# Decay attention and softplus feed-forward on one core: PSUM banks three and three, and the sign of the converted weights as a step of its own

## Chip, core and metric

The kernel runs on one core of a Trainium2 chip. The metric is the device time of one execution in microseconds; the lower the better. The engines are called as the profile calls them: PE (TensorE, with PEld for its weight loads), DVE (VectorE), ACT (ScalarE), POOL (GpSimd) and SP (SyncE, whose queue issues the DMAs).

## What is computed

Attention with a decay and a causal mask for 8 batches of 8 heads, 576 rows and 64 columns each, and then a feed-forward over the 4608 rows of 512 that come out of it:

```python
scores = scale * np.matmul(q, k.transpose(0, 1, 3, 2))
decay = cum[:, :, :, None] - cum[:, :, None, :]        # cum: running sum of log(clip(f))
scores = np.where(causal, -1000000000.0, scores + decay)
attn = softmax(scores)
x = np.matmul(attn, v)                                 # as 4608 rows of 512
h = x @ w_in                                           # 512 -> 2048
g = np.maximum(h, 0.0) + np.log1p(np.exp(-np.abs(h)))
out = g @ w_out                                        # 2048 -> 512
```

All in float32. Both weights arrive as 64-bit floats and are made into float32 in the kernel.

## The kernel before

**Order of work.** All instructions are first put into a list of operations, each with the engines that could do it, a nominal cost, what it must follow and which buffers or PSUM banks it takes and gives back. A planner (`Plan.run`) then goes through a window of 600 operations and always emits the one that can start earliest by its nominal costs. So each engine's order is fixed before the kernel runs. Where an operation may go to several engines, the planner takes the one with the smallest sum of start, cost and bias. Buffers and banks of one tag are given out in the order of the list; only the scores of attention (`loose`) may overtake, if a bank is left for the one that they pass. Where PE would stand idle for over 0.5 us before the first feed-forward accumulation, the planner puts in matmuls that nobody reads (`fill_gap`, tile `fill`, L1219).

**Weights** (`load_f64`). 32 pieces of 128x512: 16 of `w_in` (tiles `ti`, results in `woh`) and 16 of `w_out` (tiles `to`, results in `wol`). A piece is loaded (L416, 512 KB) into one of five staging buffers, of which only the two of tag `wl` serve the last twelve pieces; ACT scales its high words (L420) into a buffer of tag `fe` (four of them); POOL or DVE clips that (L423; nominal 1.57 us on POOL, and 0.34 us with a bias of 1.0 on DVE); DVE then shifts it left by three bits (L427), joins the upper bits of the low words (L431, after which the staging buffer is free for the next load) and joins the sign bit (L435, after which `fe` is free). The loads stand in SP's queue between those of q, k and v (L586 to L642).

**Attention.** Twelve jobs on plain float32 come first (four with the first 256 rows of two heads, eight with the rest of the first batch), then 56 heads in split precision. A head takes twelve PSUM banks of tag `att`: six for tiles of scores `s` (L725, L726; then DVE finds the row minimum, L730, and ACT the exponential, L750, which gives the bank back), four for turned weights `b` (L805; copied to `ph`, and DVE's L820 gives the bank back) and two for products with v, `o` (L859; given back by L886).

**Feed-forward.** 16 blocks of 256 rows and two of 512. The first works on plain float32 (L996, L1100) beside the twelve plain jobs. A unit of 512 columns of `h` fills one bank of tag `h` (L1016), goes through ACT (L1052 to L1058) and DVE (L1066), is split into `gh` and `gl` (L1074 gives the bank back), and two units later the second product runs (L1107) into banks of tag `acc`. The last two blocks use two `att` banks as well. The plain block keeps its values in buffers of tag `gh`, of which there are three, until their second product is done. Of the eight PSUM banks, `att` has four, `h` two and `acc` two.

Of the kernel before, what the change touches and what calls it, by code (L numbers as in the profile page):

```python
# [10 lines left out]
F32 = mybir.dt.float32  # L11
U32 = mybir.dt.uint32
F32R = mybir.dt.float32r
AF = mybir.ActivationFunctionType
ALU = mybir.AluOpType
# [29 lines left out]
class Plan:  # L45
# [13 lines left out]
    def add(self, on, emit, after=(), takes=(), lag=None, loose=False):  # L59
        op = Op(on, emit, after, takes, lag)  # L60
        op.loose = loose
        op.at = len(self.ops)
        self.ops.append(op)
        for t in set(takes):
            self.queue[t].append(op)
        for d in op.after:
            d.users.append(op)
        return op

    def give(self, tag, ops):  # L70

        left = [len(ops), 0.0]
        for op in ops:
            self.gives.setdefault(op, []).append((tag, left))
# [89 lines left out]
def on_act(n, more=0.0, psum=False):  # L164
    return On("ACT", (0.067 if psum else 0.095) + n / 1200 + more)


def on_dve(n, fast=False, port=False, bias=0.0):
    return On("DVE", 0.071 + n / (1920 if fast else 960), bias, fast or port)
# [39 lines left out]
def tile_decay_attention_softplus_ffn(  # L209
# [21 lines left out]
    P = 128  # L231
# [8 lines left out]
    LAG = 2  # L240
# [2 lines left out]
    QT = [(0, 64)] + [(64 + 128 * i, 128) for i in range(4)]  # L243
    QF, QR = [(0, 128), (128, 128)], [(256, 64), (320, 128), (448, 128)]

    BUFS = dict(T=2, att=4, h=2, acc=2, xs=1, fe=4, ph=3, pl=3, ph64=2, pl64=2, gh=LAG + 1, gl=LAG + 1, xh=1, xl=1,
                x32=2, wl=2, vhl=3, vraw=2, raw=1)
    plan = Plan(BUFS | dict(T0=4, stat=4, p=2, x0=1, x1=1, x2=1))
    add, give = plan.add, plan.give

    def add_dma(emit, kb, n=1, eng="SP", **more):
        return add(on_dma(kb, n, eng), emit, lag=dma_lag(kb, n, eng), **more)
# [6 lines left out]
    def bank(tag, name):  # L259
        return psum.tile([P, 512], F32, tag=tag, name=name, bufs=BUFS[tag])  # L260

    def buf(tag, shape, name, dtype=F32):
        return pool.tile(shape, dtype, tag=tag, name=name, bufs=BUFS[tag])

# [6 lines left out]
    T = {}  # L271
# [124 lines left out]
    def load_f64(src, new, name, takes=()):  # L396


        at = count["w"]
        count["w"] += 1  # L400
        stag = STAGE[at % len(STAGE)] if at < 20 else "wl"

        tag = {"xh0": "x0", "xh1": "x1", "xl0": "x2"}.get(stag, stag)
        box = {}

        def load(e):
            if stag == "wl":
                s = buf(stag, [P, NCC, TB], f"st{name}", F32R)
            else:
                x = stag[:2]  # L410
                if x not in stage_of:
                    stage_of[x] = buf(x, [P, 2, NCC, TB], f"{x}_st", F32R)
                s = stage_of[x][:, int(stag[2])]
            box["s"] = s.bitcast(U32)
            box["s"] = box["s"].rearrange("p a b -> p (a b)").rearrange("p (c t) -> p c t", t=2)
            e.dma_start(out=box["s"], in_=src)  # L416

        def scale(e):
            box["t"] = buf("fe", [P, 512], f"t{name}")
            e.activation(box["t"], box["s"][:, :, 1].bitcast(F32), AF.Copy, scale=2.0**-112)  # L420

        def clip(e):
            e.tensor_scalar(box["t"], box["t"], -HIGH, HIGH, ALU.max, ALU.min)  # L423

        def shift(e):
            x = box["x"] = new().bitcast(U32)
            e.tensor_scalar(x, box["t"].bitcast(U32), 3, None, ALU.logical_shift_left)  # L427

        def low(e):
            x, lo = box["x"], box["s"][:, :, 0]  # L430
            e.scalar_tensor_tensor(x, lo, 29, x, ALU.logical_shift_right, ALU.bitwise_or)  # L431

        def sign(e):
            x, h = box["x"], box["t"].bitcast(U32)
            e.scalar_tensor_tensor(x, h, 0x80000000, x, ALU.bitwise_and, ALU.bitwise_or)  # L435

        ld = add_dma(load, 512, after=first_rows, takes=(tag,))
        sc = add(on_act(512, 0.04), scale, after=[ld], takes=("fe",))
        on = [On("POOL", 1.57), on_dve(512, True, bias=SCALE_BIAS)]
        bt = add(on, clip, after=[sc])  # L440
        bt = add(on_dve(512, True), shift, after=[bt], takes=takes)
        bt = add(on_dve(512, port=True), low, after=[bt])
        give(tag, [bt])
        bt = add(on_dve(512, port=True), sign, after=[bt])
        give("fe", [bt])
        return bt

    def piece(x, i, dtype=F32):
# [3 lines left out]
    def load_w_in(i):  # L452
        def new():
            w_in32[i] = piece("woh", i)
            return w_in32[i]

        cc, fq = i % NCC, i // NCC
        src = w_in[cc * P : (cc + 1) * P, fq * 512 : (fq + 1) * 512]
        w_in_ready[i] = load_f64(src, new, f"i{i}")

    def load_w_out(i):
        def new():
            w_out32[i] = buf("gl", [P, DM], f"wol{i + 1}") if i == NFC - 1 else piece("wol", i + 1)
            return w_out32[i]

        takes = ("gl",) if i == NFC - 1 else ()
        w_out_ready[i] = load_f64(w_out[i * P : (i + 1) * P], new, f"o{i}", takes)
# [724 lines left out]
    att = [attention(j) for j in jobs] + [nothing, nothing]  # L1192
# [118 lines left out]
```

## Time and profile before

| | us |
|---|---|
| median of 3 runs | 1237.31 (1235.45 to 1237.55) |
| the profiled execution | 1236.16 |
| its span in the profile | 1234.4 |
| PE busy | 1214.8 (98%) |
| DVE busy | 869.1 (70%) |
| ACT busy | 870.4 (71%) |
| POOL busy | 156.5 (13%) |

Busy times of PE are made of matmuls that overlap, so 98% does not say that PE has no gaps; its `fill` matmuls count as busy as well. The stages by time: up to about 63 us the first plain jobs and two thirds of the weights, up to about 200 us the rest of the plain work, up to about 1005 us the heads in split precision with the feed-forward between them, and after that the feed-forward alone.

### The profile page before, as it was taken

The page shows a single profiled execution, that of the slowest core. Times are in us where ns is not written, and L with a number is a line of the kernel's source. Part 1 is how long each engine was busy: PE and PEld are TensorE (multiplying, and loading weights), DVE is VectorE, ACT ScalarE, POOL GpSimd, SP SyncE. Part 2 cuts the span into 40 slices and gives each one's busy share as a digit, 9 for nine tenths or more (in the row PEclk, how much of TensorE's full clock was granted, in tenths as well). Part 3 has the DMA queues.
Part 4 walks back from the last instruction along what each step waited for, and adds up shares of the span by engine and source line. Part 5 has one row for each costly group of instructions (what it writes and reads, how often), then busy time and mean ns, then how long its engine had stood idle before and what let it go on. Part 6 is the DMA issues. An engine that isn't in the chain of part 4 may idle for free.

```text
span 1234.4 us, 21512 instructions
## 1 busy us (share of the span) xinstructions
PE 1214.8 (98%) x7648; PEld 1066.9 (86%) x7648; DVE 869.1 (70%) x2175; ACT 870.4 (71%) x2069; POOL 156.5 (13%) x130
## 2 busy tenths in 40 slices
PE   8899999999999999999999999999999999999998
PEld 6666678898999999999999999999988999888887
DVE  7898999998887887676777677777778852323322
ACT  5577788978887777676776778677878754444543
POOL 4742011110110111010111001100010100000000
PEclk9899999999999999999999999999999999999999
DMA  7864534443354334343433444334434223211210
GB/s 223 262 176 133 153 92 145 128 123 119 110 152 116 121 109 117 112 130 111 118 119 95 135 118 136 99 114 118 136 102 134 73 69 103 68 52 51 86 52 35
DMA packets 53355, 143.33 MB, mean 116 GB/s; under 512 B 6656, under 2 KB 21016, under 8 KB 53248
## 3 DMA queue, kind: packets, MB, share of 16 engines
q1 hardware_dynamic: 53248, 141.95, 38.5%
q8 instruction: 61, 1.00, 0.4%
q14 instruction: 46, 0.38, 0.1%
HBM read 127.85 MB, written 14.07 MB: 115 GB/s over the span
## 4 chain that ended last, share of the span: by engine, by line
PE 74%; DVE 13%; ACT 5%; DMA 3%; issue 2%; POOL 1%; SPq 1%; DVEq 0%; ACTq 0%; POOLq 0%
PE h L1016 28%; PE acc L1107 27%; PE o L859 6%; PE b L805 6%; PE s L725 3%; PE s L726 3%; DVE s L730 2%; ACT p L773 2%; ACT p L750 1%; DMA raw<-in_qkT 1%; DVE pl L820 1%; PE acc L1100 1%; POOL ti L423 1%; DVE T L681 1%; DMA xl_st<-in_w_out 1%
## 5 line engine op out<-in xcount | busy, mean ns | idle before, releaser
L1016 PE MATMUL h<-xh,wih 128*128 128x256 f32 (+1 forms) x960 | 277.2, 312 | 0.8 <-DVE gl L1074 0.8
L1016 PE MATMUL h<-xl,wih 128*128 128x256 f32 (+1 forms) x960 | 262.9, 297 | 0.0
L1107 PE MATMUL acc<-woh_dt_float32r,gh 128*128 128x512 f32 x544 | 221.8, 408 | 0.0
L750 ACT ACTIVATE p<-s,negm 128x288 f32<-128x288 f32 (+7 forms) x384 | 183.0, 479 | 50.2 <-DVE negm L730 47.7
L1107 PE MATMUL acc<-woh_dt_float32r,gl 128*128 128x512 f32 x544 | 213.4, 392 | 0.0
L1107 PE MATMUL acc<-wol_dt_float32r,gh 128*128 128x512 f32 x544 | 213.0, 391 | 0.0
L1066 DVE SCALAR_TENSOR_TENSOR h<-h,e 128x512 f32<-128x512 f32 x136 | 95.2, 701 | 152.4 <-ACT e L1058 151.9
L775 POOL TENSOR_SCALAR p<-p,rsum 128x448 f32<-128x448 f32 (+4 forms) x77 | 97.7, 1275 | 754.7 <-DVE rsum L764 476.3
L1016 PEld LDWEIGHTS h<-xh,wih 128*128 128x128 f32 x960 | 182.7, 190 | 7.3 <-DVE gl L1074 1.2
L1016 PEld LDWEIGHTS h<-xl,wih 128*128 128x128 f32 x960 | 183.0, 191 | 5.8
L730 DVE CUSTOM_DVE_ANT_0 s<-s,cmask 128x288 f32<-128x288 f32 (+5 forms) x320 | 137.2, 438 | 54.7 <-PE s L726 46.6
L1016 PE MATMUL h<-xh,wl 128*128 128x256 f32 (+1 forms) x960 | 167.9, 297 | 0.0
L1052 ACT ACTIVATE e<-h 128x512 f32<-128x512 f32 x144 | 85.7, 595 | 111.5 <-PE h L1016 109.6
L820 DVE TENSOR_TENSOR pl<-b,ph 128x512 fp32r<-128x512 f32 (+1 forms) x224 | 125.9, 569 | 41.7 <-ACT ph L205 39.5
L805 PE MATMUL b<-ident,p 128*128 128x128 f32 x960 | 147.0, 277 | 7.9 <-ACT p L773 4.2
L1016 PEld LDWEIGHTS h<-xh,wl 128*128 128x128 f32 x960 | 138.4, 190 | 4.9
L805 PEld LDWEIGHTS b<-ident,p 128*128 128x128 f32 x960 | 112.7, 141 | 27.6 <-ACT p L773 6.5
L773 ACT ACTIVATE p<-p,rsum 128x576 f32<-128x576 f32 (+7 forms) x221 | 105.8, 542 | 28.8 <-DVE rsum L764 28.6
L1107 PEld LDWEIGHTS acc<-woh_dt_float32r,gl 128*128 128x128 f32 x544 | 102.2, 188 | 22.7
L1074 DVE TENSOR_TENSOR gl<-h,gh 128x512 fp32r<-128x512 f32 x136 | 93.6, 688 | 34.8 <-ACT gh L205 33.4
L1107 PEld LDWEIGHTS acc<-wol_dt_float32r,gh 128*128 128x128 f32 x544 | 102.9, 189 | 15.0
L1107 PEld LDWEIGHTS acc<-woh_dt_float32r,gh 128*128 128x128 f32 x544 | 102.8, 189 | 15.0
(107 smaller groups left out, 2142.8 us busy)
## 6 DMA issues: line engine op xcount, KB each, us to landing
wl<-wil_d SPq DMA_DIRECT2D x120, 512.0 KB
raw<-in_qkT SPq DMA_DIRECT2D x112, 288.0 KB
vr<-in_vR SPq DMA_DIRECT2D x64, 160.0 KB
out<-ob SPq DMA_DIRECT2D x36, 256.0 KB
sto<-in_w_out SPq DMA_DIRECT2D x11, 512.0 KB
sti<-in_w_in SPq DMA_DIRECT2D x9, 512.0 KB
wil_d<-wil SPq DMA_DIRECT2D x16, 256.0 KB
xh_st<-in_w_in SPq DMA_DIRECT2D x5, 512.0 KB
```

The lines of the kernel that those rows point to most:

```text
L730: e.tensor_tensor_reduce(out=box["o"], in0=box["o"], in1=cmask[0:n_q, right - w : right], scale=-0.125, scalar=m0 if i else 3.0e38, op0=AL ...
L750: e.activation(o, box["o"], AF.Exp, bias=m1, scale=-1.0, accum_out=acc)
L773: e.activation(a, a, AF.Copy, scale=f_)
L775: e.tensor_scalar(a, a, f_, None, ALU.mult)
L805: e.transpose(box["ps"][:, at : at + P], pt[pi][:, c : c + P], ident)
L820: e.tensor_sub(box["l"], box["ps"][:, pad : pad + w], box["h"].bitcast(F32))
L859: e.matmul(box["ps"][:, a - g0 : z - g0], st["vhl"][:, vc, :], pbox[x][:, o : o + z - a], start=i == 0 and m == 0, stop=i == len(todo) - 1 ...
L1016: e.matmul(o, l, r, start=m == 0, stop=m == 11)
L1052: e.activation(box["e"], view(st["h", fp]), AF.Abs)
L1066: e.scalar_tensor_tensor(h, h, 0.0, box["e"], ALU.max, ALU.add)
L1074: e.tensor_sub(box["l"], box["t"], box["h"].bitcast(F32))
L1107: e.matmul(st["acc"][tt], l, r[fc], start=fc == 0 and m == 0, stop=fc == NFC - 1 and m == 2,)
```

## The change

`att` gets three banks in place of four and `h` three in place of two. In the conversion of a weight piece the sign is prepared before the shift: a new step multiplies the clipped value by zero, which leaves a zero of the value's sign, in a buffer of tag `gh`. It may go to POOL or DVE with the same nominal costs as the clip. The shift then takes both tensors and joins the sign in the same instruction, and the last join is gone. `fe` and `gh` are free after the shift, the staging buffer after the join of the low words, which is now the last step.

```diff
-    BUFS = dict(T=2, att=4, h=2, acc=2, xs=1, fe=4, ph=3, pl=3, ph64=2, pl64=2, gh=LAG + 1, gl=LAG + 1, xh=1, xl=1,
+    BUFS = dict(T=2, att=3, h=3, acc=2, xs=1, fe=4, ph=3, pl=3, ph64=2, pl64=2, gh=LAG + 1, gl=LAG + 1, xh=1, xl=1,
...
+        def sign(e):
+
+            box["z"] = buf("gh", [P, 512], f"z{name}", F32R).bitcast(F32)
+            e.tensor_scalar(box["z"], box["t"], 0.0, None, ALU.mult)
+
         def shift(e):
             x = box["x"] = new().bitcast(U32)
-            e.tensor_scalar(x, box["t"].bitcast(U32), 3, None, ALU.logical_shift_left)
+            t, z = box["t"].bitcast(U32), box["z"].bitcast(U32)
+            e.scalar_tensor_tensor(x, t, 3, z, ALU.logical_shift_left, ALU.bitwise_or)
...
-        def sign(e):
-            x, h = box["x"], box["t"].bitcast(U32)
-            e.scalar_tensor_tensor(x, h, 0x80000000, x, ALU.bitwise_and, ALU.bitwise_or)
...
         bt = add(on, clip, after=[sc])
-        bt = add(on_dve(512, True), shift, after=[bt], takes=takes)
+        bt = add(on, sign, after=[bt], takes=("gh",))
+        bt = add(on_dve(512, port=True), shift, after=[bt], takes=takes)
+        give("fe", [bt])
+        give("gh", [bt])
         bt = add(on_dve(512, port=True), low, after=[bt])
         give(tag, [bt])
-        bt = add(on_dve(512, port=True), sign, after=[bt])
-        give("fe", [bt])
```

## Rows read from the trace of the kernel before

**Rows 1.** Busy time by stage: window, sum, engines (instructions), clock, DMA share, GB/s.

```profile
18.00:63.00 45.00, 38.93 (x234) 30.49 (x232) 40.95 (x97) 28.89 (x72) 29.92 (x19) 0.89 0.88 278
63.00:120.00 57.00, 55.98 (x249) 36.26 (x248) 51.02 (x135) 42.02 (x101) 20.36 (x11) 1.00 0.52 157
200.00:250.00 50.00, 48.74 (x353) 44.68 (x352) 48.61 (x130) 43.08 (x115) 6.89 (x5) 1.00 0.45 130
300.00:900.00 600.00, 599.29 (x4184) 556.03 (x4183) 449.39 (x1141) 457.61 (x1112) 64.68 (x49) 1.00 0.40 117
```

**Rows 2.** PE's unread matmuls from 18 to 63 us, groups of instructions by line.

```profile
L1219 PE MATMUL fill<-cmask 128*128 128x128 f32 x152 | 21.9, 296 | 0.0
```

**Rows 3.** Chain that ended last, from 20 to 60 us: start, length, what.

```profile
29.57 2.12 POOL to L423
...
35.09 0.60 DVE wol_dt_float L431
```

**Rows 4.** DVE's groups from 18 to 120 us: busy, mean ns, idle before.

```profile
L435 DVE SCALAR_TENSOR_TENSOR woh_dt_float<-ti,woh_dt_float 128x512 uint32<-128x512 uint32 x16 | 10.9, 685 | 0.1
...
L427 DVE TENSOR_SCALAR wol_dt_float<-to 128x512 uint32<-128x512 uint32 x15 | 7.8, 527 | 2.2 <-POOL to L423 2.2
L427 DVE TENSOR_SCALAR woh_dt_float<-ti 128x512 uint32<-128x512 uint32 x16 | 6.9, 444 | 2.4 <-POOL ti L423 2.4
```

**Rows 5.** The clip's line over the span: duration least/median/most in ns.

```profile
L423 POOL TENSOR_SCALAR to<-to x12: 1911/2067/2200, 27.4 to 111.2; 128x512 f32<-128x512 f32 x12
L423 POOL TENSOR_SCALAR ti<-ti x10: 1913/2121/2434, 18.8 to 100.5; 128x512 f32<-128x512 f32 x10
L423 DVE TENSOR_SCALAR ti<-ti x6: 411/423/884, 21.9 to 96.0; 128x512 f32<-128x512 f32 x6
L423 DVE TENSOR_SCALAR to<-to x4: 418/422/504, 51.8 to 115.8; 128x512 f32<-128x512 f32 x4
```

**Rows 6.** DVE's waits for the clip: total us, times, longest.

```profile
DVE woh_dt_float L427 <- POOL ti L423: 2.4, 4, 0.9
DVE wol_dt_float L427 <- POOL to L423: 2.2, 3, 1.4
```

**Rows 7.** Timeline: start, us, engine, line, instruction.

```profile
26.82 0.41 DVE L427 TENSOR_SCALAR woh_dt_float<-ti 128x512 uint32<-128x512 uint32 x1
27.43 8.09 POOL L423 TENSOR_SCALAR to<-to 128x512 f32<-128x512 f32 x4 [1.41 <-DVE woh_dt_float L427]
27.75 1.09 DVE L431 SCALAR_TENSOR_TENSOR woh_dt_float<-xh_st,woh_dt_float 128x512 uint32<-128x512 uint32 x1
...
87.81 0.49 DVE L763 TENSOR_SCALAR lsum<-lsum 128x3 f32<-128x3 f32 x1
```

**Rows 8.** PE's waits over the span: total us, times, longest.

```profile
PE s L725 <- ACT p L750: 3.2, 3, 1.4
...
PE b L805 <- ACT p L750: 2.0, 7, 0.4
...
PE h L1016 <- DVE gl L1074: 0.8, 2, 0.5
```

**Rows 9.** Timeline: first product with v of the first and the tenth head.

```profile
152.52 0.49 PE L859 MATMUL o<-ph,vhl 128*128 128x320 f32 x1
...
258.00 0.31 PE L859 MATMUL o<-ph,vhl 128*128 128x320 f32 x1
```

**Rows 10.** Timeline: one turned bank and one tile of scores, taken and given back.

```profile
225.62 0.77 PE L805 MATMUL b<-ident,p 128*128 128x128 f32 x5
226.14 0.38 PE L725 MATMUL s<-T 128*128 128x288 f32 x1
...
227.73 0.68 DVE L820 TENSOR_TENSOR pl<-b,ph 128x512 fp32r<-128x512 f32 x1
...
229.60 0.50 ACT L750 ACTIVATE p<-s,negm 128x288 f32<-128x288 f32 x1
```

**Rows 11.** SP's waits before a weight load: total us, times, longest.

```profile
SPq L416 <- DVE wol_dt_float L431: 29.7, 11, 6.2
```

## The prediction

> **What bounds the kernel now.** I read the busy times by stage first, then the chain that ended last, then the waits of the engines, and the timeline where a wait needed its cause.
>
> The stages have different limits [rows 1]. From 300 to 900 us PE is busy for 599.29 of 600 us: neither the banks nor the weights can gain much there, but they can lose. From 18 to 63 us PE's 38.93 us are in good part not work: 21.9 us of them are matmuls that nobody reads [rows 2]. In that stage DVE is busy for 40.95 of 45 us and the DMA engines for 0.88 of it. From 63 to 120 us DVE has 51.02 of 57 us and from 200 to 250 us 48.61 of 50 us. The chain between 20 and 60 us runs over the conversion of the weights, on DVE and on POOL [rows 3]. So up to 300 us DVE's time is what counts, and in the first 63 us a delay or a gain shows as more or less `fill`.
>
> **The weights, step by step.** There are 32 pieces, all converted between 18 and 120 us.
>
> Removed from DVE: 32 shifts in their short form. They take 7.8 + 6.9 us for 31 of them [rows 4], 15.1 us with the last one; 0.41 us each where nothing disturbs them [rows 7], 13.1 us in all. The shift in its new form reads two tensors, as the join of the sign at L435 does, which goes; the one replaces the other at 0.68 us each [rows 4], and the sum of the two is zero.
>
> Added: 32 multiplications by zero, of the clip's form, so at the clip's price: 2.07 to 2.12 us on POOL, 0.42 us on DVE [rows 5]. What the planner gives to which engine I take from the clips and from POOL's free time. Of the clips POOL got 22 of 32 [rows 5]. From 18 to 63 us POOL is busy for 29.92 of 45 us [rows 1]: 15.1 us are free, room for 7 more. From 63 to 120 us 36.6 us are free, room for all of the 13 pieces of that stage; at the share of the clips 9 go there. That makes 16 signs on POOL and 16 on DVE. The ends are all on POOL and all on DVE.
>
> DVE's saving before any side effect: 13.1 - 16 x 0.42 = 6.4 us; 13.1 us with all on POOL, and -0.3 us with all on DVE.
>
> The side effect that decides: POOL's work costs DVE time. The join at 27.75 us takes 1.09 us, where such an instruction takes 0.68 us, and it begins 0.32 us after the start of a clip on POOL [rows 7]. I count 13 such DVE instructions, of five lines, beside the 22 clips on POOL, from that one to the one at 87.81 us [rows 7]; each is 0.32 to 0.45 us longer than its like, 5.4 us together, or 0.25 us for each POOL instruction. Sixteen more on POOL cost DVE 4.0 us (32: 7.9 us; none: 0). The join at 27.75 us ended at 28.84 us, while the clip beside it, the first of four that took 8.09 us, ran to about 29.45 us [rows 7]: it waited for a part of the POOL instruction, not for its end. The Trainium skill, "SBUF — State Buffer", section "Who interferes with whom", says otherwise: whichever of a GpSimd instruction that reads SBUF and a VectorE instruction with two inputs there comes first has the shared port pair for its whole length, and the other is blocked until it ends. No row here shows so long a block; the rule's own result is the fifth rival.
>
> The second side effect: DVE waits for POOL. It did so for 2.4 + 2.2 us at L427 with 22 instructions on POOL [rows 6], 0.21 us each; 16 more make 3.3 us. The reason is that the clip's nominal price is 1.57 us and the real one 2.07 us or more: DVE's order is set by the first, and what stands behind the waiting shift in DVE's order, row minima and normalisations of the plain jobs, waits too, with PE behind them. Ends: 0 (all on DVE) and 6.7 us (all on POOL).
>
> Sum for the weights: -6.4 + 4.0 + 3.3 = +0.9 us. All on POOL: -13.1 + 7.9 + 6.7 = +1.5 us; all on DVE: +0.3 us; side effects that fall where DVE would have stood idle: down to -6.4 us.
>
> Moved with it: the staging buffer is free only after the last step, so each of the 27 later loads is issued later, by the new step's time less nothing that is gone ahead of it, up to 2.1 us. Behind a waiting load in SP's queue stand the loads of q, k and v and the decay rows of the plain jobs. SP waited for a free staging buffer for 29.7 us at the `w_out` pieces alone [rows 11] without the chain going through it for long, so I cost it at nothing; if that cover is gone, it is part of the third rival. The `gh` buffers for the signs: three, one or two of which the plain feed-forward block holds from 74 us on; a sign holds one for some 3 us (2.07 us plus the shift), pieces of that time come 57 / 13 = 4.4 us apart, so one is enough: nothing.
>
> **The banks.** What a bank costs now is seen in PE's waits [rows 8]. For the release of an `att` bank by the exponential PE waited 3.2 us at new scores and 2.0 us at turned weights, for the release of an `h` bank 0.8 us. Three in place of four for `att`: with the same queueing the first two grow by a third, 1.7 us; from below nothing, as the planner can put feed-forward matmuls there; I take 1.0 us. Three for `h`: the 0.8 us can go. Between them +0.2 us. The upper bound for `att` comes from its holding time between 150 and 260 us: ten heads begin 9 intervals apart from 152.52 to 258.00 us, 11.7 us each [rows 9]. A tile of scores held its bank from 226.14 to 230.10 us, a turned bank from 225.62 to 228.41 us [rows 10]. With 2.8 us for the products with v as well, a head holds 6 x 3.96 + 6 x 2.8 = 40.6 us of bank time, 3.5 of the four banks on the mean. Three banks give that in 13.5 us per head, 1.8 us more; for the 13 heads to 300 us that is +23 us at most. What speaks against it: the banks are held so long because their tiles queue for DVE, which is busy for 48.61 of 50 us there [rows 1]; with fewer tiles in the queue each is held for less. I take the low end, as DVE's busy share is the nearer row.
>
> **Sum.** The profiled execution took 1236.16 us (span 1234.4 us and 1.8 us around it). +0.9 and +0.2 us give 1237.3 us; the median lies 1.15 us above that execution, so the forecast is 1238.4 us, or no change that can be measured. About 0.2% is what a measurement of this kernel can tell from no change. The forecast's own range is 1234 to 1241 us.
>
> **Rivals.**
>
> First, faster: the planner, which sees 6.4 us less on DVE, orders the first 63 us better, and the stretched instructions fall beside the chain. Then 6.4 us and up to two of the 3.3 us of waits are won: 1237.3 - 6.4 - 1.5 = 1229.4 us. For it: 21.9 us of `fill` to be won, and DVE on the chain. Against it: POOL is on the chain as well [rows 3].
>
> Second, faster: the third `h` bank lets PE run feed-forward matmuls wherever attention is late. PE's idle time by the rows of its stages is 1.0 us from 63 to 120 us and 1.3 us from 200 to 250 us [rows 1], so some 2% of the 180 us from 120 to 300 us and a like share of the last heads, 6 us in all: 1231.3 us. Against it: only 0.8 us of waits on `h` are seen.
>
> Third, slower: POOL sets the pace of the first stage. If the planner gives POOL both steps of each of the 14 pieces that it clips up to 63 us, that is 28 x 2.1 = 58.8 us in a stage of 45 us, 13.8 us too much; DVE's order waits for half of it, as the other half lies beside DVE's own work: 1244.3 us. It decides from the point where POOL's free 15.1 us are used up, 7 signs. For it: the nominal price, which is 0.5 us too low for each instruction. Against it: the planner turns to DVE when POOL has a queue.
>
> Fourth, slower: the three `att` banks do stretch the heads from 150 to 300 us. A third of the upper bound is 8 us: 1245.3 us. It decides where the mean need of banks, 3.5, stays above three. For it: the 5.2 us of waits on `att` with four banks. Against it: DVE's queue, as said.
>
> Fifth, slower: a POOL instruction keeps a DVE instruction with two inputs waiting until it ends. The shift is now such an instruction, and the joins are. One that begins at a random point of a sign waits 1.0 us, half of 2.07 us; 16 of them cost 16.6 us in place of 4.0 us: 1251.0 us. Against it: the 13 stretched instructions wait 0.45 us at most. This is the rule of the Trainium skill's page on SBUF named above.
>
> That the change doesn't do what it says could only be that the planner puts nearly all signs on DVE; that is in the forecast's range.
>
> **How the numbers follow.** Forecast 0.30, first rival 0.25, second 0.10, third 0.14, fourth 0.18, fifth 0.03. Within 0.2% of 1237.31 us (1234.8 to 1239.8 us) lies most of the forecast, with 0.02 of it below and 0.01 above: faster 0.37, same 0.27, slower 0.36. The range that should hold the time 8 times in 10 takes in the centres of the first four rivals, and stops short of both faster ones together (1223 us) and both slower ones together (1251 us): 1226 to 1248 us.
>
> **What would show it.** Right: the multiplications by zero some half on POOL and half on DVE; 15 to 25 DVE instructions stretched by 0.3 to 0.5 us before 120 us; DVE's waits for POOL of 6 to 10 us; `fill` from 18 to 63 us at about 22 us; the heads from 150 to 260 us still under 12 us apart; from 300 us on PE as full as now. The first rival is seen in `fill` under 16 us and an earlier start of the plain feed-forward; the second in less idle PE time from 120 to 300 us; the third in `fill` over 27 us with DVE waiting for POOL at the new shift; the fourth in heads of 12.5 us or more and more of PE's waits on L750. Wrong it would be above all if the planner's new order moves the plain jobs against the weights by more than the terms here, since each engine's order is made anew by any change of cost.

## The result and the profile after

Over seven runs of each on the same chips the kernel before took 1236.66 us (median, 1235.45 to 1238.41) and the changed kernel 1239.77 us (1238.41 to 1241.7): a ratio of 1.0028 with an interval of 1.0018 to 1.0038. The change costs 0.28%, a little more than the 0.2% that can be told from nothing. All times are medians of executions with a mean granted clock of 0.99 or more; one execution each of e2_sign and d2_att2 and one of the kernel before ran at 0.75 to 0.85 and are left out. The profiled execution of the changed kernel has a span of 1238.0 us (before 1234.4 us) with a mean granted clock of 0.997 (before 0.994); from 300 to 900 us it is 1.00 in both. Line numbers behind the new step are three higher than before (L725 is L728, L750 is L753, L805 is L808).

Busy time by stage in the changed kernel, to be laid beside [rows 1] with the same columns:

```profile
18.00:63.00 45.00, 39.34 (x225) 29.89 (x225) 42.80 (x96) 32.42 (x84) 34.66 (x23) 0.94 0.86 257
63.00:120.00 57.00, 55.87 (x243) 35.79 (x242) 51.21 (x132) 39.95 (x94) 22.17 (x14) 1.00 0.56 173
200.00:250.00 50.00, 49.59 (x337) 44.29 (x336) 44.57 (x122) 41.91 (x108) 6.40 (x5) 1.00 0.44 125
300.00:900.00 600.00, 598.27 (x4150) 551.00 (x4151) 453.41 (x1149) 460.83 (x1129) 65.42 (x51) 1.00 0.41 118
```

The first column, PE's busy time, has hardly moved anywhere. The loss is in the last row, and in the columns beside it: from 300 to 900 us there are 34 matmuls fewer (4150 in place of 4184) and 5.0 us less of weight loads (551.00 in place of 556.03 us), while "busy" fell by 1.0 us only. At 600 us for 4184 matmuls, 34 of them are 4.9 us on the mean, more than the 3.6 us by which the span grew.

The unread matmuls from 18 to 63 us, to be laid beside [rows 2]:

```profile
L1222 PE MATMUL fill<-cmask 128*128 128x128 f32 x131 | 20.7, 302 | 0.0
```

The clip (L423) and the new sign step (L428) by engine, to be laid beside [rows 5] (least, median and most ns of one):

```profile
L423 DVE TENSOR_SCALAR ti<-ti x10: 414/428/875, 18.7 to 98.3; 128x512 f32<-128x512 f32 x10
L423 DVE TENSOR_SCALAR to<-to x10: 408/428/878, 29.1 to 120.4; 128x512 f32<-128x512 f32 x10
L423 POOL TENSOR_SCALAR to<-to x6: 1926/2114/2294, 33.9 to 73.4; 128x512 f32<-128x512 f32 x6
L423 POOL TENSOR_SCALAR ti<-ti x6: 1923/2264/2460, 43.6 to 101.5; 128x512 f32<-128x512 f32 x6
...
L428 POOL TENSOR_SCALAR zo<-to x10: 1488/1746/1980, 30.0 to 121.0; 128x512 f32<-128x512 f32 x10
L428 DVE TENSOR_SCALAR zi<-ti x9: 407/427/823, 19.3 to 103.6; 128x512 f32<-128x512 f32 x9
L428 POOL TENSOR_SCALAR zi<-ti x7: 1488/1497/1860, 23.5 to 98.9; 128x512 f32<-128x512 f32 x7
L428 DVE TENSOR_SCALAR zo<-to x6: 407/427/828, 36.3 to 116.6; 128x512 f32<-128x512 f32 x6
```

Signs: 17 on POOL, 15 on DVE. But of the clips POOL now has 12 in place of 22. POOL's conversion work is 29 instructions in place of 22, not 38, and DVE has 35 of the short ones (20 clips, 15 signs) in place of 42 (10 clips, 32 short shifts).

DVE's waits for POOL from 18 to 125 us, beside [rows 6] (total us, times, longest):

```profile
DVE zi L428 <- POOL ti L423: 1.4, 1, 1.4
DVE wol_dt_float L433 <- POOL zo L428: 0.9, 2, 0.5
DVE woh_dt_float L433 <- POOL zi L428: 0.5, 1, 0.5
DVE zo L428 <- POOL to L423: 0.2, 1, 0.2
```

PE's waits over the span on the banks, beside [rows 8], and the first product with v of the first and of the tenth head, beside [rows 9]:

```profile
PE b L808 <- ACT p L753: 3.5, 9, 0.8
...
PE s L726 <- ACT p L753: 1.4, 3, 0.9
...
PE h L1019 <- DVE gl L1077: 0.2, 1, 0.2
```

```profile
157.77 0.39 PE L862 MATMUL o<-ph,vhl 128*128 128x320 f32 x1
...
275.34 0.39 PE L862 MATMUL o<-ph,vhl 128*128 128x320 f32 x1
```

The heads now begin 117.57 / 9 = 13.06 us apart; before it was 11.72 us.

### An account of PE's time

"Busy" does not show what is lost, because a matmul's record runs on while the next one has begun. The distance from one start to the next does. This is the timeline of PE in the changed kernel (start, us, engine, line, instruction):

```profile
336.39 0.28 PE L1019 MATMUL h<-xh,wih 128*128 128x256 f32 x1
336.51 0.28 PE L1019 MATMUL h<-xl,wih 128*128 128x256 f32 x1
336.80 0.39 PE L728 MATMUL s<-T 128*128 128x320 f32 x1
```

The first distance, 0.12 us, is that of such a matmul when nothing stops it. The second is 0.29 us: 0.17 us went by before the scores could begin, and all but 0.01 us of it hides in a "busy" of 0.28 us. I did this for every matmul of the span: its distance to the next start, less the distance of its kind in the kernel before when undisturbed (the one that a fifth of them stay below; for the single-precision kinds the median). What is left is called a gap here. `fill` is the distance that the unread matmuls take up. Span less `fill` less gaps comes out at 1127.4 to 1128.5 us in all kernels below, so the two account for their differences to about 1 us. In us:

```
kernel        att/h sign step  span    fill  gaps 0-63  63-300  300-900  900 on
before         4/2   no        1234.4  37.9     4.6      24.6     28.3    10.7
e2_sign        4/2   yes       1232.1  28.5     6.8      29.8     28.5    10.1
s1_sign_dve    4/2   DVE only  1235.3  38.3     3.8      25.7     28.3    10.7
n1_lag         4/2   no        1238.5  39.9     2.6      28.2     28.6    11.0
n2_sign_lag    4/2   yes       1236.0  28.5     8.4      31.8     28.3    10.7
n5_lag2        4/2   no        1231.3  38.0     4.4      22.3     28.5     9.8
after          3/3   yes       1238.0  35.4     4.9      24.5     34.8    10.4
e1_banks       3/3   no        1243.8  40.1     4.1      26.8     35.0    10.2
n3_banks_lag   3/3   no        1238.4  39.9     3.4      22.1     35.4     9.9
n4_both_lag    3/3   yes       1242.4  44.9     3.7      20.9     34.6    10.1
e3_att3        3/2   no        1246.7  39.1     4.5      29.8     35.3    10.6
e4_sign_att3   3/2   yes       1239.7  35.9     4.8      25.1     35.2    10.8
```

Each row is one profiled execution; with the 1.8 us around its span it lies up to 2.2 us from the median of its kernel, so differences of 2 us between two rows alone prove little. Between before and after: +6.5 us from 300 to 900 us, -2.5 us of `fill`, and 0.3 us or less elsewhere. The size hangs a little on what is taken as undisturbed: with the median for every kind the same step is +5.7 us, with the distance that a tenth stay below +7.9 us. Three and four banks stand apart with each of them.

The two kernels do not run the same mix in that stretch. As the heads come later, the changed kernel has 1575 matmuls of attention there in place of 1536, and 2575 of the feed-forward in place of 2645. That is not what makes the gaps: at the gaps of before after a matmul of each sort the new mix would have 0.5 us less of them. What grew is the gap after a matmul of scores, from 7 to 14 ns on the mean.

### The profile page after: what moved, and what is told of

The parts are those of the page before. It is cut to its first block, busy times and chain, and to the rows that moved or that the text cites. A ratio compares the mean times of both kernels' runs of the same rounds, so it can differ in the third digit from the quotient of the medians.

```text
span 1238.0 us, 21502 instructions
## 1 busy us (share of the span) xinstructions
PE 1217.8 (98%) x7622; PEld 1062.6 (86%) x7622; DVE 873.2 (71%) x2159; ACT 875.7 (71%) x2080; POOL 162.4 (13%) x135
## 4 chain that ended last, share of the span: by engine, by line
PE 76%; DVE 13%; ACT 4%; DMA 3%; issue 2%; POOL 1%; SPq 0%; DVEq 0%; POOLq 0%; ACTq 0%
PE h L1019 28%; PE acc L1110 27%; PE b L808 7%; PE o L862 6%; PE s L728 3%; PE s L729 3%; DVE s L733 2%; ACT p L776 1%; DVE T L684 1%; ACT p L753 1%; DVE T L690 1%; DMA sto<-in_w_out 1%; DVE pl L823 1%; DMA sti<-in_w_in 1%; DMA raw<-in_qkT 1%
## 5 line engine op out<-in xcount | busy, mean ns | idle before, releaser
L753 ACT ACTIVATE p<-s,negm 128x288 f32<-128x288 f32 (+7 forms) x384 | 182.9, 479 | 56.3 <-DVE negm L733 54.9
L808 PE MATMUL b<-ident,p 128*128 128x128 f32 x960 | 142.4, 275 | 6.9 <-ACT p L753 3.5
L808 PEld LDWEIGHTS b<-ident,p 128*128 128x128 f32 x960 | 111.6, 140 | 28.9 <-ACT p L753 8.7
L776 ACT ACTIVATE p<-p,rsum 64x64 f32<-64x64 f32 (+6 forms) x226 | 107.4, 539 | 29.4 <-DVE rsum L767 28.4
```

What stands on the lines that cost most here:

```text
L753: e.activation(o, box["o"], AF.Exp, bias=m1, scale=-1.0, accum_out=acc)
L776: e.activation(a, a, AF.Copy, scale=f_)
L808: e.transpose(box["ps"][:, at : at + P], pt[pi][:, c : c + P], ident)
```

## The experiments

Two explanations stood against each other at first: that the banks cost time and the sign step gives some back, or that neither does much and the planner's new order decides. The planner makes one list of all engines' instructions from nominal costs, so any edit changes the order of everything behind it.

### One part alone

**e1_banks**: the kernel before with the new bank counts only.

```diff
-    BUFS = dict(T=2, att=4, h=2, acc=2, ...
+    BUFS = dict(T=2, att=3, h=3, acc=2, ...
```

> Three attention banks and three banks for the first product, with the weights converted as before. Bank theory (the attention banks stretch the heads up to 300 us): the first ten heads 13.1 us apart as in the changed kernel, fill from 18 to 63 us as before (21.9 us), time 0.4% to 0.6% over before, 1241 to 1244 us. Sign theory (the conversion costs the time): no change, heads 11.7 us apart. Order theory (any new order of the instructions moves the time by some us either way): a time within 0.4% of before that says nothing of either part.

Measured: 1244.82 us, a ratio of 1.0074 (1.0062 to 1.0086). The banks alone cost 0.7%, more than the whole change. The bank theory is the nearest of the three, but the heads are further apart than it said (14.0 us in place of 13.1 us) and the time lies just above its range.

**e2_sign**: the changed kernel with the old bank counts.

```diff
-    BUFS = dict(T=2, att=3, h=3, acc=2, ...
+    BUFS = dict(T=2, att=4, h=2, acc=2, ...
```

> The new conversion of the weights alone, with four attention banks and two for the first product. Bank theory: heads 11.7 us apart as before, fill 2 to 3 us less, time 0.2% under before, some 1234 us. Sign theory: slower than before by about what the whole change costs, 1240 us, with DVE waiting for POOL. Order theory: within 0.4% of before, either way.

Measured: 1236.00 us, 1.0003 (0.9994 to 1.0012). The sign step alone does nothing that can be measured, and the sign theory falls with it. The bank theory's details do not hold here: the heads are 12.4 us apart, and `fill` falls by more than the 2 to 3 us that it said. The windows of the two, in the columns of [rows 1]; first the banks alone:

```profile
200.00:250.00 50.00, 44.27 (x292) 40.01 (x291) 41.90 (x111) 36.65 (x93) 3.33 (x4) 0.93 0.40 123
300.00:900.00 600.00, 598.31 (x4153) 550.87 (x4153) 453.47 (x1157) 461.32 (x1132) 66.97 (x52) 1.00 0.39 117
```

then the sign step alone:

```profile
200.00:250.00 50.00, 45.55 (x310) 40.83 (x309) 44.05 (x123) 38.94 (x104) 7.00 (x6) 0.97 0.39 114
300.00:900.00 600.00, 599.27 (x4176) 555.32 (x4174) 448.91 (x1142) 457.80 (x1111) 65.83 (x50) 1.00 0.39 118
```

From 300 to 900 us the banks alone do what the changed kernel does, 4153 matmuls and 550.87 us of weight loads; the sign step alone leaves both nearly as they were. So the loss behind 300 us belongs to the banks. Ahead of 300 us the sign step alone won 9.4 us of `fill`:

```profile
L1222 PE MATMUL fill<-cmask 128*128 128x128 f32 x96 | 13.1, 286 | 0.0
```

(21.9 us in [rows 2]), and lost most of it again: gaps grew by 2.2 us up to 63 us and by 5.2 us from there to 300 us. The chain that ended last, of the sign step alone, from 195 to 255 us (start, length, what), shows where: 25.5% of it are loads of q and k for a next head into the single `raw` buffer.

```profile
198.84 5.05 DMA raw<-in_qkT
...
238.73 5.95 DMA raw<-in_qkT
...
248.33 4.31 DMA raw<-in_qkT
```

Such loads are not the sign step's own doing. The same chain has them in n1_lag (below), which has the old conversion in another order, for 21.9% of these 60 us:

```profile
227.78 4.28 DMA raw<-in_qkT
...
242.34 4.55 DMA raw<-in_qkT
...
254.64 4.30 DMA raw<-in_qkT
```

They are also in n2_sign_lag, and in none of the other nine kernels of the table, s1_sign_dve with the new conversion among them.

### Which bank, and how many

**e3_att3**: the kernel before with three banks for attention and still two for `h`. **e4_sign_att3**: the changed kernel in the same way.

```diff
-    BUFS = dict(T=2, att=4, h=2, acc=2, ...
+    BUFS = dict(T=2, att=3, h=2, acc=2, ...
```

> Three attention banks, two for the first product, one bank unused, conversion as before. Bank theory: heads 13 us apart, slower than with the third bank for the first product or equal to it: 1242 to 1246 us; what lies between the two is what the third bank gives back. If that third bank is what costs the time, this one is like before, 1237 us.

> The changed kernel with two banks in place of three for the first product (one bank unused). If the third bank gives something back, 1242 us or more; if it gives nothing, the changed kernel's 1239.8 us; if it is harmful, under 1238 us. Heads 13 us apart by the bank theory in any case.

Measured: 1247.63 us, 1.0091 (1.0078 to 1.0105), over the 1242 to 1246 us expected, and 1239.53 us, 1.0030 (1.0018 to 1.0041). The third `h` bank won at most 2.8 us without the sign step (1247.63 to 1244.82 us, with intervals that overlap) and nothing with it (1239.53 to 1239.77 us); from 300 to 900 us the gaps are the same with two as with three (35.3 and 35.2 against 35.0 and 34.8 us). So the loss there comes from the fourth `att` bank, and the third `h` bank doesn't pay for it.

**d2_att2**: two for attention and four for `h`. **d3_att5**: five and one.

```diff
-    BUFS = dict(T=2, att=4, h=2, acc=2, ...
+    BUFS = dict(T=2, att=2, h=4, acc=2, ...     (d3_att5: att=5, h=1)
```

> The kernel before with two attention banks and four for the first product. Bank theory: the step from four to three took the first ten heads from 11.7 to 14.0 us apart, so the step to two goes on at least as far: 17 to 21 us apart, and 1265 to 1300 us. If instead the heads' distance in the three-bank kernels came from a chance order of the instructions, two banks need not be worse than three: under 1250 us.

> The kernel before with five attention banks and one for the first product. Bank theory: the first ten heads as close as before or closer, 11 to 11.7 us, as DVE is full with four banks already. The single bank for the first product makes units wait for the one ahead, in the last 230 us above all (7.4 us a unit in place of 5.5 us for 32 units): 1290 to 1320 us. If a bank for attention is no limit at four, a fifth leaves the heads' distance where it is.

Measured: 1344.16 us, 1.0885 (1.0864 to 1.0906), and 1338.17 us in a single execution, where before had a median of 1234.77 us. Both are slower than expected (1265 to 1300 us and 1290 to 1320 us). Going from three `att` banks to two costs some 100 us, from four to three at most 12 us: the kernel before stood just above the point at which the banks bind hard. What a fifth `att` bank is worth the second run doesn't tell, since it goes with a single `h` bank; its heads are 12.2 us apart, no closer than before.

### Order alone

**n1_lag** and **n5_lag2** change a nominal delay of the planner by a few per cent, in the kernel before: the time until PE sees another engine's result, and the time until a given-back buffer can be taken. No instruction is added or removed, only the order moves.

```diff
-PELAG, GLAG, PORTLAG = 0.1, 0.2, 0.09
+PELAG, GLAG, PORTLAG = 0.105, 0.2, 0.09     (n5_lag2: 0.1, 0.205, 0.09)
```

> The kernel before with nothing changed but a nominal delay of the planner, 0.105 us in place of 0.100 us, which makes a new order of the same instructions. It measures what a new order alone is worth. Order theory: 0.3% or more from before, either way, as much as the whole change. Bank theory: within 0.2% of before, heads 11.5 to 12.5 us apart.

> The kernel before with another nominal delay, 0.205 us in place of 0.200 us for giving back a buffer: a second sample of what a new order alone does. Between 1230 and 1243 us; weight loads from 300 to 900 us at 555 to 556 us, as it has four banks; any difference arises before 300 us.

Measured: 1240.68 us, 1.0051 (1.0032 to 1.0070), and 1233.76 us, 0.9988 (0.9979 to 0.9996). Order alone moves this kernel by +0.51%, more than the change did, and by -0.12%; the second is faster than both kernels, and by nothing but luck of order. Its gaps from 300 to 900 us are those of before (28.5 us); nearly all that differs between the three orders lies ahead of 300 us.

So each part was tried again under the other order. **n2_sign_lag**, **n3_banks_lag** and **n4_both_lag** are e2_sign, e1_banks and the changed kernel with this one line as in n1_lag:

```diff
-PELAG, GLAG, PORTLAG = 0.1, 0.2, 0.09
+PELAG, GLAG, PORTLAG = 0.105, 0.2, 0.09
```

> The new conversion with four and two banks, under the nominal delay of 0.105 us: with the next two kernels a repeat of the four combinations in another order of the instructions. If a new order alone moves the early part by 0.3% to 0.5%, this one lies anywhere within 0.6% of before, 1228 to 1243 us. From 300 us on it is like the other four-bank kernels, whose weight loads there took 555.3 to 556.0 us in 600 us.

> Three and three banks, the old conversion, nominal delay of 0.105 us. If three attention banks cost a fixed amount after 300 us whatever the order, the weight loads from 300 to 900 us come to 550 to 551 us, as in the four three-bank kernels so far, not 555 to 556 us; the loss there is 6 to 7 us. The time as a whole then is 6 us over the same order with four banks, give or take what the early part does: 1238 to 1250 us.

> The changed kernel under the nominal delay of 0.105 us. Fixed cost of three banks after 300 us: 550 to 551 us of weight loads from 300 to 900 us again. If the conversion is what takes back 5 us wherever there are three banks, it is 5 us faster than the same without it; if that was chance of the order, the two differ by anything up to 6 us either way.

Measured against before: 1238.12 us, 1.0029 (1.0018 to 1.0039); 1241.23 us, 1.0051 (1.0038 to 1.0065); 1242.04 us, 1.0055 (1.0043 to 1.0068). Against n1_lag, the kernel with this delay and neither part, these ratios put the sign step at -0.22%, the banks at 0.00% and both together at +0.04%; with the first delay it was +0.03%, +0.74% and +0.28%. The interval of n1_lag alone is 0.19% to either side, so the three differences from it are good to about 0.2% and not clear of zero. n3_banks_lag has the 550 to 551 us of weight loads that were expected, but not the 6 us over the same order with four banks; n4_both_lag, with 551.59 us, lies just above those. Two effects repeat under both orders, two do not:

- The 6 to 7 us behind 300 us repeat in every kernel with three banks: 34.6 to 35.4 us of gaps in six of them, 28.3 to 28.6 us in the six with four. The windows of n3_banks_lag, whose whole time is no longer than n1_lag's, have them as well:

```profile
300.00:900.00 600.00, 597.86 (x4145) 550.12 (x4144) 452.57 (x1147) 461.40 (x1130) 65.91 (x51) 1.00 0.39 118
```

- With four banks the sign step shortens `fill` to 28.5 us under both orders, and gaps take most of it back (63 to 300 us: +5.2 and +3.6 us).
- What the banks do ahead of 300 us does not repeat: `fill` and gaps up to there sum to 64.8 to 73.4 us with three and to 64.7 to 70.7 us with four. The means are 68.3 and 67.4 us.
- That the sign step wins with three banks does not repeat: the same sum falls by 6.2 us from e1_banks to the changed kernel and by 7.6 us from e3_att3 to e4_sign_att3, and rises by 4.1 us from n3_banks_lag to n4_both_lag.

A good part of what does not repeat is PE's clock. In e3_att3 the granted clock was at half from 214.7 to 228.4 us and in e1_banks from 222.6 to 229.4 us; in e4_sign_att3 and the changed kernel it was full from 63 to 900 us. The same stretch in e3_att3 and then in e4_sign_att3, in the columns of [rows 1]:

```profile
214.70:228.40 13.70, 11.00 (x46) 9.51 (x46) 11.14 (x32) 8.01 (x22) 1.41 (x1) 0.50 0.26 68
214.70:228.40 13.70, 13.70 (x103) 12.74 (x103) 12.77 (x35) 12.85 (x34) 1.41 (x1) 1.00 0.35 97
```

The gaps in it come to 8.7 us in e3_att3, more than the whole 7.6 us between these two, and some 5.5 us of them are the clock's (an estimate: half of PE's 11.00 us). In e1_banks the gaps at half clock come to 2.7 us. From 300 to 900 us the clock was 1.00 in all twelve kernels, so the loss there has nothing to do with it.

### What shortens the fill

**s1_sign_dve**: e2_sign with the sign step on DVE only.

```diff
-        bt = add(on, sign, after=[bt], takes=("gh",))
+        bt = add(on[1:], sign, after=[bt], takes=("gh",))
```

> The new conversion with four attention banks and two for the first product, the multiplication by zero on DVE only. By the forecast's prices this is worth nothing against the kernel before (32 short instructions go, 32 come): 1235 us, fill from 18 to 63 us near 20 us. If what shortened the fill is work that POOL takes over, the fill is back at 20 us or more; if it is the shorter chain of a piece or the planner's new order, it stays near the 13 us seen with the signs half on POOL.

Measured: 1236.58 us, 1.0011 (1.0000 to 1.0021). `fill` from 18 to 63 us is back near the 21.9 us of before:

```profile
L1222 PE MATMUL fill<-cmask 128*128 128x128 f32 x142 | 20.0, 289 | 0.0
```

With four banks the new sequence by itself does not shorten it, then; POOL's share goes with it. In e2_sign POOL has 34 instructions of the conversion and in n2_sign_lag 31, with 28.5 us of `fill` in both; in the other four POOL has 20 to 22, with 37.9 to 39.9 us. In the changed kernel and in e4_sign_att3 POOL has 29 and `fill` lies between (35.4 and 35.9 us). But n4_both_lag has 28 and the longest `fill` of all, 44.9 us: with three banks POOL's share does not decide it, and what does was not isolated.

Why a head's q and k come late in e2_sign, n1_lag and n2_sign_lag was not isolated either. A second `raw` buffer would tell; no kernel here has one.

## Why the prediction was right, and where it was wrong

The forecast of 1238.4 us lies 1.4 us below the measured 1239.77 us and inside its own range of 1234 to 1241 us. It called for no change that can be measured, with +1.1 us; measured are +3.1 us, just beyond that bound. The total is near in good part by luck: the term for the `att` bank was far too small, the weights, forecast as a small loss, were a small gain at most, and order alone moves this kernel by -0.12% to +0.51%, a spread of twice the measured change.

**Signs on POOL, -6.4 us on DVE.** 16 of 32 forecast, 17 measured: right, and on DVE their price too (0.427 us at the median, 0.42 us forecast). On POOL the clip's price was taken, 2.07 to 2.12 us; a single multiplication takes 1.50 to 1.75 us. What the step missed is that the planner also moves the clips: ten of them went back to DVE. So DVE has 7 short instructions fewer, not 16, and saves 7 x 0.42 = 2.9 us.

**The stretch, +4.0 us.** The size was right: between 18 and 125 us 25 DVE instructions beside a clip or a sign on POOL are over 0.25 us longer than their like, 9.4 us in all; the same count gives 14 and 5.8 us in before. That is +3.6 us, and 25 lies at the end of the 15 to 25 that were forecast. It came from fewer POOL instructions (7 more, not 16) at a higher price (9.4 / 29 = 0.32 us in place of 0.25 us each). Over the twelve kernels of the table the count follows POOL's: 10 to 16 stretched with 20 to 23 POOL instructions, 19 to 25 with 28 to 34. With it DVE's conversion comes to 66.6 us of busy time in place of 64.1 us: 2.9 us less for the short instructions, and some 5 us more by which instructions of the conversion itself run longer.

That a POOL instruction blocks to its end, the fifth rival and the rule of the Trainium skill, "SBUF — State Buffer", section "Who interferes with whom", is not borne out. The timeline of the changed kernel has the new two-input shift inside a sign and inside a clip on POOL:

```profile
29.96 1.79 POOL L428 TENSOR_SCALAR zo<-to 128x512 f32<-128x512 f32 x1 [0.43 <-DVE to L423]
30.32 1.09 DVE L433 SCALAR_TENSOR_TENSOR woh_dt_float<-ti,zi 128x512 uint32<-128x512 uint32 x1
...
33.94 2.29 POOL L423 TENSOR_SCALAR to<-to 128x512 f32<-128x512 f32 x1
34.37 1.09 DVE L433 SCALAR_TENSOR_TENSOR wol_dt_float<-to,zo 128x512 uint32<-128x512 uint32 x1
```

The first began 0.36 us after the sign did and ended at 31.41 us, 0.34 us before the sign's end; the second ended 0.77 us before the clip's. Each took 0.41 us more than its 0.68 us, though POOL ran on. No shift of the kernel took over 1.10 us.

**DVE's waits for POOL, +3.3 us.** Wrong in sign: forecast 6 to 10 us in all, measured 3.0 us (the four rows above) in place of 4.6 us, as POOL had fewer clips and shorter signs. The third rival, POOL setting the pace, goes with it: its mark was `fill` over 27 us from 18 to 63 us, and that came out at 20.7 us (forecast about 22 us).

**The weights in all, +0.9 us.** With these sizes the same sum is -2.9 + 3.6 - 1.6 = -0.9 us. On the chip the sign step with four banks was worth nothing measurable in one order and 0.22%, some 2.7 us and hardly clear of noise, in the other; `fill` and gaps to 300 us fell by 2.0 us in both. The first rival is half seen: with four banks `fill` falls as it says (13.1 us, under its 16 us), but the time comes back as later gaps, and with three banks it hardly falls.

**The `att` banks, +1.0 us.** This is the step that failed. Measured are 6.5 us from 300 to 900 us. I had named the loss ("they can lose") but priced the bank by PE's waits and looked for it between 150 and 260 us only; from 300 us on I forecast PE as full as before. PE's waits from 300 to 900 us are these (total us, times, longest), the first line of before and the other two of the changed kernel:

```profile
PE b L805 <- ACT p L750: 0.4, 1, 0.4
PE b L808 <- ACT p L753: 1.1, 3, 0.4
PE s L728 <- DVE x L889: 0.2, 1, 0.2
```

They grew from 0.4 to 1.3 us, where the gaps grew by 6.5 us: a view that lists waits sees only those in which PE's record had ended. The gaps that grew are those after matmuls of scores and of attention otherwise: from one score to the next they sum to 2.8 us from 300 to 420 us and to 2.7 us from there to 900 us; in before to 0.8 and 1.7 us. That is 3.0 of the 6.5 us; the rest is spread over the other changes between kinds. What shows the loss are the columns of weight loads and counts beside PE's busy time.

**The heads.** Forecast under 12 us apart, measured 13.06 us; in the other kernels with three banks 12.9 to 14.0 us, with four 11.7 to 12.6 us. The means are 13.4 and 12.2 us, and 13.5 us is what the prediction worked out for three banks. So the mean need of 3.5 banks [rows 9, 10] did decide, as the fourth rival said, and my reason against it, that DVE's 48.61 of 50 us [rows 1] is the limit anyway, fell: DVE is busy there for 44.57 us now, for 41.90 us with the banks alone, and for 44.05 us in e2_sign with four. But the fourth rival's price was wrong as well. The later heads cost no PE time by themselves: gaps from 63 to 300 us are 24.5 us in place of 24.6 us, as PE had feed-forward matmuls for the time between. In n3_banks_lag they are 6.1 us smaller than in n1_lag, which is how that kernel wins back all of its loss behind 300 us.

**The `h` bank, -0.8 us.** PE's wait fell from 0.8 us to 0.2 us, as forecast; worth at most 2.8 us in one pair and nothing in another. The second rival, feed-forward in PE's idle time from 120 to 300 us, is not seen: PE is idle for 3.7 us there, before 3.6 us.

**Two sums of the rivals.** The fifth rival's 1251.0 us starts from the median of 1238.4 us; from 1237.3 us, as in the other four, it is 1249.9 us. The third and fourth together are 1252 us, not 1251 us. Neither moves the forecast or its range.

**What stays open.** The 6.5 us behind 300 us are shown to come from the missing `att` bank; which release each late score waited for is not. Whether the 2.5 us of `fill` against them belong to the sign step or to the order cannot be told: kernels that differ in order alone spread by 6 us ahead of 300 us. So the sign of the whole, +3.1 us, holds for this order; in the other one the same change came out at +0.04%. The prediction named this, each engine's order made anew by any change of cost, as what would make it wrong above all, and gave it no number.

## What to carry to other kernels

Where PE looks fully busy, look at its weight loads and the number of matmuls of a long stretch, or at the distances between starts: a missing bank shows there as some 1% fewer matmuls and weight loads while "busy" stays at 99.5% or more. Count a buffer by its mean need against the number at hand (3.5 of 4 here), and if the need lies above the new number, price it in every stage in which such tiles run, not only where waits are seen. And where a planner makes the order, run the same kernel with a nominal cost moved by some per cent before a difference of half a per cent is put down to an edit.

## What the runs showed of the hardware

- A `tensor_scalar` of 128x512 in f32 takes POOL 1.91 to 2.46 us with two operations (max and min) and 1.49 to 1.98 us with one (a multiplication); on DVE both take 0.41 to 0.43 us undisturbed.
- Where a DVE instruction is held up beside a POOL instruction, it ends at one of a few distances from POOL's end: 0.33 to 0.34 us or 0.77 us before it for the two-input ones of 0.68 us (11 cases of the changed kernel), and 0.60 to 0.61 us or 1.02 to 1.03 us before, or 0.27 to 0.28 us after it, for the short ones of 0.41 us (9 cases). Those before it lie some 0.43 us apart, and no wait was longer than 0.5 us in any of the twelve kernels. The profile calls its spans on POOL rough; that these distances repeat to 0.01 us speaks for them here. That POOL lets DVE in at steps of this length would fit; it was not tested.
- The granted clock of these executions is at one of two levels, 1.00 or 0.50 (2.4 and 1.2 GHz), and the 0.93 of e1_banks from 200 to 250 us is a mean of the two. It fell to half at 214.7 us in e3_att3 after PE had been busy for 3.55 of 5.7 us, and at 222.6 us in e1_banks after 3.67 of 5.6 us. PE's busy time of a whole stage does not tell it: the changed kernel kept 1.00 from 250 to 300 us with 47.79 us busy, and before had 0.97 there with 48.72 us.
